# Hash attention and a SwiGLU block: three moved pieces of work at the seam between the two halves

## The chip, the cores and the metric

The kernel runs on one core of one Trainium2 chip. The metric is the device time of one execution in microseconds (us). Four runs of the kernel before gave 958.33, 955.05, 956.46 and 951.87 us, a median of 955.76.

## The reference, cut to what matters

```python
# q, k, v: (4, 8, 768, 64); proj: (64, 6)
q_bits = (q @ proj) > 0; k_bits = (k @ proj) > 0        # six sign bits a row
mask = (bucket(q_bits)[:, :, :, None] == bucket(k_bits)[:, :, None, :])
scores = where(mask, q @ k.T / 8, -1e9)
attn = softmax(scores) @ v                              # float32
x = attn, laid out as (4 * 768, 512)
g = x @ w_gate                                          # 512 x 1536, given as float64
out = ((g * sigmoid(g)) * (x @ w_val)) @ w_out          # 1536 x 512
```

The weights arrive as float64, and the matmuls of the second half are done to nearly float32 accuracy: each operand is cut into a high part, a low part and their difference, so that every product costs three matmuls.

## The kernel before, in words

**Two halves on one core.** `attention` goes over 16 pairs of heads (4 batches of 4 pairs, n = 0 to 15; `NP` = 4). `gated_block` then goes over the 4 batches: for each, twelve up blocks (`("U", f)`, 128 columns of both w_gate and w_val) and four down products (`("D", n)`, three up blocks' worth of w_out). Their order is written out in `order`: U0 U1 U2 U3 D0 U4 U5 U6 D1 U7 U8 U9 D2 and so on.

**A pair of attention.** TensorE (PE) makes scores in 24 groups (line 471), ScalarE (ACT) takes the exponentials (474), VectorE (DVE) adds them up (503, 507), PE multiplies by v (485). The sums of a pair are made one pair later by `total`: four pairs of matmuls with ones (518), a copy to `row` (521) and a small DMA few<-row (523) on SP's queue. `invert` takes reciprocals and spreads them by way of DRAM (sums, then r, 536); `norm` scales x by them (542, DVE), and for batches 1 to 3 sends x to DRAM (xram<-xT, 547). The lists `waiting`, `last` and `left` carry these closures on to later places. From pair 4 on the next pair's q and k are transposed on DVE (438); their hash bits go through ACT (402) and a spread (411 on DVE for k, a DMA qb<-qb, 414, on SP for q).

**Preparing the weights.** w_gate, w_val and w_out are cut into 36 pieces of 128 by 512 numbers. A piece goes through: a load (`words`, line 122); two scalings on ACT (130, 131); three steps on DVE (`widths`: 144, 146, 149); a rounding on ACT (137, `round_up`); two steps on DVE (`parts`: 157, 159); and a write to DRAM, ram<-stage (161), 768 KB. The stage tile of a piece is one of three buffers (four in attention), so the scaling of piece i waits until the write of piece i - 3 has landed. 24 pieces are prepared within attention, by `begin_pieces(count)` and `advance_pieces` once a pair; the other 12 within the first batch of the gated part. There the generator `preparing` hands out one DVE step at a time (five for each piece), and `scale_ahead` issues the scalings of the next piece when the counts allow.

**The gated part.** A prepared piece comes back to SBUF by a ring load, ring<-ram (232), 768 KB, issued by GpSimd; the ring has seven tiles, and `bring` loads the next one when one has been used. An up block makes, for gate and then for value, 16 matmuls into `a` and 8 into `n` (both at line 632). ACT evicts `a` (674), DVE subtracts `n` (680); silu on ACT (682), a product on DVE (684), and hid is cut into parts by ACT (685) and DVE (688, 690, the `tail`). A down product goes over six chunks; a chunk is six matmuls into `t[:, 0]` and three into `t[:, 1]`, which are evicted by ACT (719, first product of a batch) or DVE (721) and then a subtraction on DVE (724). All these PSUM tiles (a, n, o) come from one pool of four, taken in turn.

**What sets the order.** There is no scheduler: each engine runs its instructions in the order in which Python issues them. In the gated part one "atom" is issued (an up block's half, or a chunk), then the tail of the block before, then one preparing step, then `scale_ahead`:

```python
            for atom in atoms_of(kind, n):
                tail = atom()
                finish(tails)
...
                prepare_on(1)
                scale_ahead()
```

Ahead of U9 of a batch (`f == NF - NQ`) the next batch's x is fetched into the buffers that `words` used, so all preparing steps that are left are issued there in one go:

```python
                if f == NF - NQ and b + 1 < B:
                    while next(preparing, None):
                        pass
```

In the last down product of all, the first two thirds of four chunks are issued ahead (`ahead = 4`), and the rest of each chunk after them.

Of the kernel before, what the change touches and what calls it, by code (L numbers as in the profile page):

```python
# [13 lines left out]
ALU = mybir.AluOpType  # L14
# [5 lines left out]
def kernel(  # L20
# [35 lines left out]
    NQ = 3  # L56
# [108 lines left out]
    def begin_pieces(count):  # L165
        for i in sorted(added - rounded):
            round_up(i)
        for i in range(progress["scaled"], min(progress["scaled"] + count, NPIECE)):
            load_words(i + 1)
            scale(i)  # L170
# [50 lines left out]
    def bring(count=1):  # L221
        for _ in range(count):
            i = len(held)
            if i == len(wanted):
                return
            what, n = wanted[i]
            at = place[what, n % NF]
            while progress["kept"] <= at:
                next(preparing)
            pool = ringp[i % sum(RINGS) >= RINGS[0]]  # L230
            held[what, n] = t = pool.tile([P, 3, PIECE], FP32R, tag="ring", name="ring")
            nc.gpsimd.dma_start(t.bitcast(FP32), ram[at].bitcast(FP32))  # L232
# [23 lines left out]
    def attention(scope):  # L256
# [306 lines left out]
        for n in range(len(pairs)):  # L563
            u = 2 * NCH * n
            more = n + 1 < len(pairs)
            late = n + 1 > NP
            if n and more:
                steps = front(n + 1)
                if late:
                    prepare_pair(2)  # L570
            for i in range(2 * NCH):
                score(u + i)
                if u + i == 2:
                    prepare_pair(1)
                    finish(rest)
                    steps = front(n + 1)
                if i % NCH:
                    add(u + i)
                if late and i == 2:
                    load(n + 2, "qk")  # L580
            if more and not late:
                prepare_pair(4)
                load(n + 2, "qk")
            if n:
                total(n - 1)
            if more:
                prepare_pair(1)
            finish(rest)
            finish(last)
            while waiting:  # L590
                last.append(waiting.pop(0)())
            begin_pieces(0 if n == len(pairs) - 1 else 2 if n < NP or n % 2 else 1)
            for c in range(NCH):
                attend(u + c)
            finish(splits)
            for c in range(NCH, 2 * NCH):
                attend(u + c)
            load(n + 2, "v")
            advance_pieces()
            if n >= len(pairs) - 3:  # L600
                bring(2 if n == len(pairs) - 1 else 1)
        finish(last)
        total(len(pairs) - 1)
        left.extend(waiting)

    left = []
# [8 lines left out]
    def gated_block(scope):  # L615
# [47 lines left out]
        def atoms_of(kind, n):  # L663
            if kind == "U":
                b = n // NF
                hid = hids[n] = hidp.tile([P, 3, S], FP32R, tag="hid", name="hid")
                h, l, d = (hid[:, i] for i in range(3))
                gate, val = (gatep.tile([P, S], FP32, tag=name, name=name) for name in "gv")
                ops = {}
                for what, z in (("g", gate), ("v", val)):  # L670
                    def one(what=what, z=z):
                        ops[what] = up(n, what)
                        ops[what][0]()
                        nc.scalar.activation(two(z), ops[what][2], AF.Copy, scale=STEP + 1)  # L674

                    def other(what=what, z=z):
                        _, second, _, n_ = ops[what]
                        second()
                        bring()
                        nc.vector.tensor_tensor(two(z), two(z), n_, op=ALU.subtract)  # L680
                        if what == "g":
                            nc.scalar.activation(z, z, AF.Silu)  # L682
                            return
                        nc.vector.tensor_tensor(val, gate, val, op=ALU.mult)  # L684
                        nc.scalar.activation(h, val, AF.Copy, scale=TOWARD / STEP)  # L685

                        def tail():
                            nc.vector.scalar_tensor_tensor(out=l, in0=h.bitcast(FP32), scalar=-STEP,  # L688
                                                           in1=val, op0=ALU.mult, op1=ALU.add)
                            nc.vector.tensor_tensor(d, h.bitcast(FP32), l.bitcast(FP32),  # L690
                                                    op=ALU.subtract)

                        return tail

                    yield one
                    yield other
            else:
                b, part = divmod(n, NF // NQ)
                ws = [held["o", NQ * n + j] for j in range(NQ)]
                hs = [hids[NQ * n + j] for j in range(NQ)]  # L700
                tiles = {}

                def start(c, js):
                    if c not in tiles:
                        tiles[c] = two_banks("o")
                    t = tiles[c]
                    cols = slice(c * P, (c + 1) * P)
                    for j in js:
                        for v in range(2):
                            mm(t[:, 0], hs[j][:, v, cols], ws[j][:, v],  # L710
                               j == 0 and v == 0, j == NQ - 1 and v == 1)
                    for j in js:
                        mm(t[:, 1], hs[j][:, 2, cols], ws[j][:, 2], j == 0, j == NQ - 1)

                def end(c):
                    t = tiles.pop(c)
                    if part == 0:
                        accs[c] = outp.tile([P, DM], FP32, tag=f"o{c}", name="o")
                        nc.scalar.activation(accs[c], t[:, 0], AF.Copy, scale=STEP + 1)  # L719
                    else:  # L720
                        nc.vector.scalar_tensor_tensor(out=accs[c], in0=t[:, 0],  # L721
                                                       scalar=STEP + 1, in1=accs[c],
                                                       op0=ALU.mult, op1=ALU.add)
                    nc.vector.tensor_tensor(accs[c], accs[c], t[:, 1], op=ALU.subtract)  # L724
                    if part == NF // NQ - 1:
                        nc.sync.dma_start(rows[b][:, c, :], accs[c])
                    if c == NCH - 1:
                        bring(NQ)

                ahead = 4 if n == B * NF // NQ - 1 else 0  # L730
                for c in range(ahead):
                    yield lambda c=c: start(c, range(NQ - 1))
                for c in range(NCH):
                    def chunk(c=c):
                        start(c, [NQ - 1] if c < ahead else range(NQ))
                        end(c)
                    yield chunk
# [6 lines left out]
        for kind, n in order:  # L744
            if kind == "U":
                b, f = divmod(n, NF)
# [3 lines that stand above are left out]
                    splits = [None] * 4  # L750
                    for pr in range(NP):
                        t = wordp.tile([P, PIECE, 2], I32, tag="words", name="words")
                        x = t.rearrange("p f w -> p (f w)")[:, 0:S].bitcast(FP32)
                        nc.sync.dma_start(x, kept_x[b + 1, pr])
                        splits += split(x, b + 1, pr, xs[(b + 1) % 2][pr])
            if kind == "D" and n == B * NF // NQ - 1:
# [4 lines that stand above are left out]
                if tail:  # L761
                    tails.append(tail)
                if splits:
                    step = splits.pop(0)
                    if step:
                        step()
                count[0] += 1
                if left and count[0] in (6, 14):
                    left.append(left.pop(0)())
                    left[:] = [f for f in left if f]  # L770
                prepare_on(1)
                scale_ahead()

    with ExitStack() as scope:
# [33 lines left out]
```

## Time and profile before

| | |
|---|---|
| median of four runs | 955.76 us |
| the profiled execution: its own time, its span | 958.33 us, 956.6 us |
| TensorE busy | 928.3 us, 97% of the span, 5413 matmuls |
| VectorE busy | 672.8 us, 70% |
| ScalarE busy | 472.9 us, 49% |
| mean granted TensorE clock | 0.995 |
| DMA | 203.22 MB, a mean of 212 GB/s |
| attention | 0 to 340.66 us (first gated matmul) |
| first batch's D0, D1, D2 | from 378.02, 415.52 and 460.76 us |

The profile is one execution. "Busy" counts an engine's instructions, not its waits; a wait is written in square brackets behind the instruction that had to wait, with what released it. In a table of stretches, the figures behind the start and end are the length, the busy time of PE, its weight loads, DVE, ACT and GpSimd, then the granted PE clock, the share of the DMA engines and GB/s. In the chain, a line gives start, length and what it was.

### The profile page before, as it was taken

The numbers are of one execution on the slowest core, as the hardware profiler recorded it, in microseconds if no ns is written. First come the engines' busy times: TensorE is split into PE (matmuls) and PEld (weight loads), VectorE is DVE, ScalarE is ACT, GpSimd is POOL, SyncE is SP. The second block draws the span as 40 slices with busy tenths as digits, with TensorE's granted clock in tenths as the row PEclk, the third lists the DMA queues.
The fourth block names the chain that finished last, engine by engine and source line by source line (L and its number), as shares of the span: only waits on it lengthen the run. The fifth ranks groups of instructions, "written<-read, shape, count | busy, mean of one in ns | idle before, by whom it ended". The sixth has DMA issues, their size and how long they took to land.

```text
span 956.6 us, 14590 instructions
## 1 busy us (share of the span) xinstructions
PE 928.3 (97%) x5413; PEld 728.9 (76%) x5413; DVE 672.8 (70%) x868; ACT 472.9 (49%) x882; POOL 113.2 (12%) x231
## 2 busy tenths in 40 slices
PE   8999999999999999999799999999999999999997
PEld 3444455444554478989599999999999999999996
DVE  5577899888898828787876546775646586446466
ACT  6899777887887735534242331332332422332311
POOL 3011001000011020111011011011111111110100
PEclk9999999999999999999899999999999999999999
DMA  6466667888788598879677475466654645753641
GB/s 166 124 187 177 182 169 197 216 207 185 199 228 210 191 342 293 320 266 362 236 247 280 163 255 182 166 239 221 257 200 158 234 183 196 267 198 132 240 156 66
DMA packets 135798, 203.22 MB, mean 212 GB/s; under 512 B 92912, under 2 KB 100560, under 8 KB 135728
## 3 DMA queue, kind: packets, MB, share of 16 engines
q0 software_dynamic: 27984, 145.64, 43.0%
q1 hardware_dynamic: 106944, 56.46, 22.3%
q8 instruction: 43, 0.70, 0.3%
q10 hardware_dynamic: 800, 0.20, 0.1%
q14 instruction: 27, 0.22, 0.1%
HBM read 162.01 MB, written 39.42 MB: 211 GB/s over the span
## 4 chain that ended last, share of the span: by engine, by line
PE 65%; DVE 12%; SPq 8%; DMA 7%; ACT 4%; issue 4%; DVEq 0%; ACTq 0%; POOLq 0%
PE a L632 22%; PE o L632 18%; PE n L632 11%; PE sc L471 8%; SPq L296 7%; PE av L485 4%; DMA ram<-stage 3%; DVE acc L507 2%; ACT A L474 1%; DVE o L724 1%; DMA qb<-qb 1%; DVE stage L146 1%; DMA r<-sums 1%; DVE stage L157 1%; PE hps L397 1%
## 5 line engine op out<-in xcount | busy, mean ns | idle before, releaser
L632 PE MATMUL a<-xparts,ring 128*128 128x384 f32 x1536 | 282.6, 335 | 3.7 <-ACT g L674 2.7
L632 PEld LDWEIGHTS a<-xparts,ring 128*128 128x128 f32 x1536 | 267.9, 188 | 6.6 <-ACT g L674 3.3
L632 PE MATMUL o<-ring,hid 128*128 128x512 f32 x864 | 201.7, 393 | 7.5 <-ACT g L674 7.4
L632 PEld LDWEIGHTS o<-ring,hid 128*128 128x128 f32 x864 | 162.8, 189 | 42.5 <-ACT g L674 7.7
L474 ACT ACTIVATE A<-sc 128x384 f32<-128x384 f32 x384 | 156.1, 508 | 14.0 <-PE sc L471 13.9
L471 PE MATMUL sc<-qT,kT 64*128 64x384 f32 x768 | 160.2, 492 | 0.0
L632 PE MATMUL n<-xparts,ring 128*128 128x384 f32 x768 | 148.6, 335 | 0.0
L232 POOL DMA_DIRECT2D ring<-ram x144 | 75.9, 529 | 511.9 <-PE n L632 313.9
L632 PEld LDWEIGHTS n<-xparts,ring 128*128 128x128 f32 x768 | 134.5, 188 | 0.0
L507 DVE TENSOR_TENSOR acc<-acc,A 128x768 f32<-128x768 f32 x128 | 122.7, 958 | 13.7 <-DVE acc L503 0.5
L485 PE MATMUL av<-A,vraw 128*64 128x386 f32 (+1 forms) x768 | 127.7, 489 | 0.0
L680 DVE TENSOR_TENSOR v<-v,n 128x768 f32<-128x768 f32 x48 | 45.8, 954 | 101.8 <-PE n L632 95.9
L471 PEld LDWEIGHTS sc<-qT,kT 64*128 64x128 f32 x768 | 75.3, 188 | 49.6 <-issue 45.6
L485 PEld LDWEIGHTS av<-A,vraw 128*64 128x64 f32 x768 | 53.7, 137 | 73.3 <-issue 63.8
L674 ACT ACTIVATE g<-a 128x768 f32<-128x768 f32 x48 | 38.8, 808 | 127.9 <-PE a L632 127.9
L685 ACT ACTIVATE hid<-v 128x768 fp32r<-128x768 f32 x48 | 40.6, 847 | 117.7 <-DVE v L684 111.0
L682 ACT ACTIVATE g<-g 128x768 f32<-128x768 f32 x48 | 40.7, 847 | 92.1 <-DVE g L680 92.1
L471 PE MATMUL sc<-qb,kb 64*128 64x384 bf16 x384 | 73.5, 325 | 8.9 <-DVE kb L411 4.8
L724 DVE TENSOR_TENSOR o<-o 128x512 f32<-128x512 f32 x96 | 66.0, 687 | 22.0 <-ACT o L719 19.5
L688 DVE SCALAR_TENSOR_TENSOR hid<-hid,v 128x768 fp32r<-128x768 f32 x48 | 45.9, 957 | 31.6 <-ACT hid L685 31.6
L680 DVE TENSOR_TENSOR g<-g,n 128x768 f32<-128x768 f32 x48 | 45.6, 949 | 31.2 <-PE n L632 29.8
L721 DVE SCALAR_TENSOR_TENSOR o<-o 128x512 f32<-128x512 f32 x72 | 49.5, 687 | 12.0 <-PE o L632 11.4
(77 smaller groups left out, 672.8 us busy)
## 6 DMA issues: line engine op xcount, KB each, us to landing
ring<-ram POOLq DMA_DIRECT2D x144, 768.0 KB, 5.6
ram<-stage POOLq DMA_DIRECT2D x24, 768.0 KB, 4.5
ram<-stage SPq DMA_DIRECT2D x12, 768.0 KB
vraw<-in_v_dram SPq DMA_DIRECT2D x16, 384.0 KB
out_dram<-o SPq DMA_DIRECT2D x24, 256.0 KB
r<-sums SPq DMA_DIRECT2D x30, 192.0 KB
qraw<-in_q_dram SPq DMA_DIRECT2D x48, 96.0 KB
words<-in_moe_w_gate_dram POOLq DMA_DIRECT2D x9, 512.0 KB, 7.5
```

The costliest lines, as they stand in the source:

```text
L232: nc.gpsimd.dma_start(t.bitcast(FP32), ram[at].bitcast(FP32))
L296: queue.dma_start(blocks[at : at + BLOCK], src[b, 2 * pr + h][:, x * BLOCK : (x + 1) * BLOCK].rearrange("(a p c) d -> p c a d", c=NCH, p=B ...
L471: nc.tensor.matmul(sc[h], x["k", n][rows, ks], x["q", n][rows, qs], start=start, stop=not start)
L474: nc.scalar.activation(weights(u)[:, h, 0:HQ], sc[h], AF.Exp, scale=SCALE * (OFF / 2 if n <= NP else 1.0))
L485: nc.tensor.matmul(ps[h * D : (h + 1) * D, 0:width], raws["v", n][:, h, c, :], a[:, h, 0:width], start=c == 0, stop=c == NCH - 1)
L507: nc.vector.tensor_tensor(acc[n, half], acc[n, half], a[:, :, 0:HQ], op=ALU.add)
L632: nc.tensor.matmul(ps, w, x, start=start, stop=stop)
L680: nc.vector.tensor_tensor(two(z), two(z), n_, op=ALU.subtract)
L682: nc.scalar.activation(z, z, AF.Silu)
L688: nc.vector.scalar_tensor_tensor(out=l, in0=h.bitcast(FP32), scalar=-STEP, in1=val, op0=ALU.mult, op1=ALU.add)
L721: nc.vector.scalar_tensor_tensor(out=accs[c], in0=t[:, 0], scalar=STEP + 1, in1=accs[c], op0=ALU.mult, op1=ALU.add)
L724: nc.vector.tensor_tensor(accs[c], accs[c], t[:, 1], op=ALU.subtract)
```

## The change

There are four edits. `begin_pieces` starts one piece in pair 5 instead of two, and two in pair 6 instead of one; the sum over all pairs stays at 24. After the last pair, `total(15)` is issued ahead of `finish(last)`, which holds the scaling of x of pair 14 (`norm`) and its DMA to DRAM; on SP, few<-row then stands ahead of xram<-xT. Beside a chunk of a down product two preparing steps are issued instead of one. And in the very last down product each chunk issues its three difference matmuls (`t[:, 1]`) ahead of the other six, and DVE subtracts them ahead of the scaled addition of `t[:, 0]`. No instruction is added or taken away on PE, DVE, GpSimd or SP; lines move by 6 to 10 in the later part of the file.

```diff
-            begin_pieces(0 if n == len(pairs) - 1 else 2 if n < NP or n % 2 else 1)
+            begin_pieces(0 if n == len(pairs) - 1 else 2 if n < NP or n % 2 and n > NP + 1 or n == NP + 2 else 1)
...
+        total(len(pairs) - 1)
         finish(last)
-        total(len(pairs) - 1)
         left.extend(waiting)
...
                     cols = slice(c * P, (c + 1) * P)
-                    for j in js:
-                        for v in range(2):
-                            mm(t[:, 0], hs[j][:, v, cols], ws[j][:, v],
-                               j == 0 and v == 0, j == NQ - 1 and v == 1)
-                    for j in js:
-                        mm(t[:, 1], hs[j][:, 2, cols], ws[j][:, 2], j == 0, j == NQ - 1)
+                    def first():
+                        for j in js:
+                            for v in range(2):
+                                mm(t[:, 0], hs[j][:, v, cols], ws[j][:, v],
+                                   j == 0 and v == 0, j == NQ - 1 and v == 1)
+
+                    def second():
+                        for j in js:
+                            mm(t[:, 1], hs[j][:, 2, cols], ws[j][:, 2], j == 0, j == NQ - 1)
+
+                    for go in (second, first) if final else (first, second):
+                        go()
 
                 def end(c):
                     t = tiles.pop(c)
+                    if final:
+                        nc.vector.tensor_tensor(accs[c], accs[c], t[:, 1], op=ALU.subtract)
                     if part == 0:
...
-                    nc.vector.tensor_tensor(accs[c], accs[c], t[:, 1], op=ALU.subtract)
+                    if not final:
+                        nc.vector.tensor_tensor(accs[c], accs[c], t[:, 1], op=ALU.subtract)
...
-                ahead = 4 if n == B * NF // NQ - 1 else 0
+                final = n == B * NF // NQ - 1
+                ahead = 4 if final else 0
...
-                prepare_on(1)
+                prepare_on(2 if kind == "D" else 1)
                 scale_ahead()
```

## The prediction

> **What bounds the kernel now.** I read the page first, then PE's waits, the order in time around them, and the chain.
>
> ```profile
> span 956.6 us, 14590 instructions
> PE 928.3 (97%) x5413; PEld 728.9 (76%) x5413; DVE 672.8 (70%) x868; ACT 472.9 (49%) x882; POOL 113.2 (12%) x231
> ```
>
> PE is busy for 928.3 of 956.6 us, so only the 28 us in which it stands still, and its slow stretches, can be won. From 475 us PE runs without a pause to 951; what matters lies before. PE's waits between 340 and 480 us:
>
> ```profile
> PE o L632 <- ACT g L674: 7.4, 1, 7.4
> PE a L632 <- ACT g L674: 2.7, 2, 2.5
> ```
>
> The first of them, in order of time:
>
> ```profile
> 456.59 0.66 ACT L130 ACTIVATE stage<-words 128x512 f32<-128x512 f32 x1 [4.01 <-DMA ram<-stage]
> ...
> 459.92 0.79 ACT L674 ACTIVATE g<-a 128x768 f32<-128x768 f32 x1
> 460.76 14.55 PE L632 MATMUL o<-ring,hid 128*128 128x512 f32 x54 [7.41 <-ACT g L674]
> ```
>
> At U9 (the tenth of the first batch's twelve up blocks) the code runs all preparing steps that are left, in one go. ACT stands in order behind scalings (L130), each waiting until a piece's write to DRAM (ram<-stage) frees one of three stage buffers; the eviction of g is behind them, and PE waits for it from 453.35 to 460.76: 7.4 us. The next 54 matmuls take 14.55 us where the later sets of the chain take 12.28, because the clock fell:
>
> ```profile
> 458.00:460.76 2.76, 0.00 (x0) 0.00 (x0) 2.59 (x5) 1.66 (x3) 0.00 (x0) 0.50 0.86 274
> 460.76:465.00 4.24, 4.24 (x10) 2.88 (x11) 3.90 (x5) 0.24 (x1) 0.00 (x0) 0.52 0.90 332
> ```
>
> PEclk (the seventh figure) is 0.50 from about 4.6 us after PE stopped until 465. The jam costs 7.4 + 2.3 = 9.7 us.
>
> The second wait is at the start of the gated part:
>
> ```profile
> 348.52 0.32 SPq L547 DMA_DIRECT2D xram<-xT  x1
> 348.94 0.59 SPq L523 DMA_DIRECT2D few<-row  x1
> 358.47 0.84 ACT L685 ACTIVATE hid<-v 128x768 fp32r<-128x768 f32 x1 [6.67 <-DMA words<-in_moe_w_out_dram]
> 360.06 3.05 PE L632 MATMUL a<-xparts,ring 128*128 128x384 f32 x16 [2.47 <-ACT g L674]
> ```
>
> The first hid tile lies where attention's tiles were, and by the program's waits its first writer needs both of these DMAs landed (the view guesses a third). The landing records give 355.29 for xram<-xT and 358.29 for few<-row; ACT goes on at 358.47, and PE lost 2.47 us.
>
> **The change, part by part.** The sum is against the profiled execution (958.33 us, span 956.6 and 1.7 around it), 2.6 us above the median of the four runs, 955.76; I carry the difference over to the median. Runs of one kernel spread over 951.87 to 958.33, so 0.5% (4.8 us) is about what can be told from no change.
>
> *One piece from pair 5 to pair 6.* DVE then does three widths steps less at the end of pair 5 (144, 146, 149: 1.78 us from 145.38 to 147.16). PE's wait for kb at 160.24 (1.49 us) goes. But pair 7 gets two parts steps more (1.33 us) before its transposes; the q and k loads on SP stand behind the transposes and the spread of qb behind those, and PE waits for qb at 180.70 (0.90 us) and 200.75 (0.51 us). By pair 9 the chain is where it was: 0, with -1.2 to +0.7 us for the range.
>
> *Sums ahead of the scaling of x.* few<-row then leaves at 340.7, when row is copied (340.13 + 0.48), instead of behind the scaling that waits until 347.48 for r. On SP it stands ahead of xram<-xT only; both are on one queue and it is 6 KB. hid then waits for xram<-xT alone: 355.3, 3.0 us earlier. ACT's g is out at 357.0, PE ends its block at 357.6 and does not wait: -2.5 us, and part of the two small waits behind (0.40 and 0.22): -2.9 us, from -2.4 to -3.1.
>
> *Differences first in the last down product.* In both orders DVE's first step on a chunk waits for the chunk's last matmul (the program sets one semaphore count for the whole tile), and two DVE steps of 0.69 us follow. Nothing is won at the end. PE needs the hid's difference (ready at 944.07) at the first late matmul instead of the third, but the 24 matmuls ahead end at 944.46. Cost 0; if that cover failed, about 0.4 us.
>
> *Steps doubled beside down products.* In the changed order D0 and D1 carry six steps more each, and of the jam's twelve DVE steps one remains. The jam goes: -9.7 us. So does D1's wait of 0.5. What comes instead I follow along the changed order, with the durations of before (spacing on DVE 0.60 for 128x512, 1.0 for 128x768).
>
> D0 (PE 378.02 on). Before the second chunk's subtraction stand two steps, so it ends at 388.9, not 388.3; the sixth chunk needs its PSUM tile: +0.6 us, and D0 ends at 391.2. ACT's round-up of a piece now stands ahead of the eviction of the fourth chunk and waits for a step that ends at 391.1. So the fourth chunk is done on DVE at 393.1, and the step behind it ends piece 27, which SP sends off at 393.75 (ram<-stage; before at 395.47). Now the crucial order: behind the sixth chunk ACT has the scaling of piece 30, which needs the buffer of piece 27, and only behind it the eviction of U4's g. Before, that eviction stood ahead of the scaling. PE goes through U4 until 399.55 and then needs that PSUM tile.
>
> When does piece 27 land? The three ring loads of 768 KB that D0's end releases leave at 391.2. Rows of before for a write that leaves soon after such a triple:
>
> ```profile
> 395.47 13.13 DMA ram<-stage
> 430.43 6.84 DMA ram<-stage
> 437.26 3.82 issue
> ```
>
> 13.1 us for one sent 4.9 us behind the triple, 10.6 us (landing record 441.01, ACT goes on at 441.08) for one 2.2 us behind it. Without a triple it is short: sent at 388.94, landed 392.18, 3.24 us. Piece 27 now leaves 2.55 us behind the triple; I take 10.6, with ends 3.2 and 13.1. It lands at 404.35; the two scalings (start to start 0.57 each, with waits 1.2) and the eviction (0.80) bring PE to 406.4: +6.9 us. As after the jam, the clock falls 4.6 us into that wait and stays low for 6.8: +2.3 us.
>
> The Trainium skill, DMA: Bandwidth & Descriptors, section Queues, rings and completion order, says that each engine takes turns between the queues that have work. By that a 768 KB write beside ring loads at half of some 400 GB/s would take an estimated 4 us and about 2 of latency, land at about 400, and cost some 2 us with no fall of the clock; the sum would be some 7 us lower. The rows of before differ: between 392.5 and 396.5 the DMA moved 366 GB/s, and by the packet records all of it was ring loads, while a load that SP had issued at 392.32 had not begun.
>
> D1. The wait in U5 lets DVE catch up, so its six chunks come in time. Piece 32 is ready 15.3 us into D1, 3 us behind the next triple, and with 10.6 lands at 25.9. ACT's scaling of piece 35 waits for it, and behind it stand 0.57 + 0.57 of scaling, silu (0.85) and v's eviction (0.80); PE wants v's tile at 25.2 and gets it at 28.8: +3.6 us, and 0.4 for U8's first tile. Ends 0 and 6.
>
> Sum: -9.7 - 0.5 - 2.9 + 0.6 + 6.9 + 2.3 + 4.0 = +0.7 us. Of the median: 956.5 us.
>
> **The rivals.**
>
> *Writes land in time* (faster). If HBM writes in D0 land in 3.2 us as the one at 388.94 did, U5 costs nothing: -9.2. Then DVE has not caught up at D1: by the same counting the sixth chunk waits 1.6, U7's tiles 0.4, 1.1 and about 1.5, +4.6, and U8 about 1.5 instead of 4.0. Sum +0.7 - 9.2 + 4.6 - 2.5 = -6.4: 949.4 us. For it: the DMA stands idle from 386.5 to 389.5 (share 0.06), and the next load of words leaves with the triple, not behind it. Against: both rows behind a triple took over 10 us.
>
> *The jam moves and grows* (slower). One mechanism: ACT stands in order behind a scaling whose buffer is not free. With 13.1 us for piece 27 (lands 406.9) U5's wait is 2.5 us longer, though PE then starts later in the slow stretch (-1.3); with the same for piece 32, U8's wait is 6.1, over 4.6, and the clock falls there too (2.6): +0.7 + 2.5 - 1.3 + 2.5 + 2.6 = +7.0: 962.8 us. It decides where landings take over some 11.6 us, from which U8's wait passes 4.6. For it: the row of 13.13 us. Against: PE that stands issues no ring loads, so the queue empties sooner than it did before.
>
> *Only the sums count.* If the step order did as much harm as good exactly, what stays is the -2.9 of the sums: 952.9 us, within the bound; it is part of the first case.
>
> **How the numbers follow.** An even trade, within 4.8 us either way, 0.45: the big terms, 13.1 off and 13.8 on, come from one mechanism (ACT behind a scaling) and are of one size. Landing in time 0.31: it needs one duration that no row behind a triple shows, but every smaller stall leans that way, and the sums' gain is nearly sure. Grown jam 0.24. The range: from 2 us below the faster case, for pair 6's 1.2 and part of the D1 stalls, 947; to 963, near the slower case; some 2 in 10 lie outside. The likeliest case's own range is 951.7 to 961.
>
> **What would show it.** Right: PE's wait of 7.4 for g at the third D is gone and its 54 matmuls take 12.3 us; ACT's hid goes on near 355.3; a wait of PE for g's eviction of some 7 us at U5, with PEclk 0.50 behind it, and in the chain ram<-stage of about 10 us ahead of it; a shorter one at U8. The last 54 matmuls and the two DVE steps behind them are unchanged. Wrong: no wait of PE over 2 us between D0 and D1 (then the faster case), or hid still held to 358 (then few<-row was not what held it), or two falls of the clock.

## The result, and the profile after

The changed kernel takes 958.18 us (median of 53 runs, 955.40 to 960.91), the kernel before 955.00 us (79 runs, 950.44 to 960.41): the ratio is 1.0032, with a 95% interval from 1.0024 to 1.0040. The change costs about 3 us and stays within the 0.5% that count here as no change. The two profiled executions alone would say the opposite, 956.45 us after and 958.33 before: single executions of one kernel differ by more than the change is worth, so medians are compared below, and profiles are read by stretches.

PE's waits after, from 335 to 480 us (us in total, times, longest):

```profile
PE a L632 <- ACT g L674: 7.9, 3, 6.2
PE a L632 <- ACT v L674: 3.7, 2, 3.4
```

The wait of 7.4 us ahead of D2 is not there; two others are. In the order of time (start, length, the operation, and in brackets the wait ahead of it):

```profile
334.94 0.59 SPq L523 DMA_DIRECT2D few<-row  x1
343.90 0.32 SPq L547 DMA_DIRECT2D xram<-xT  x1
...
351.60 0.84 ACT L685 ACTIVATE hid<-v 128x768 fp32r<-128x768 f32 x1 [4.44 <-DMA xram<-xT]
353.20 3.07 PE L632 MATMUL a<-xparts,ring 128*128 128x384 f32 x16 [1.48 <-ACT g L674]
...
397.14 0.66 ACT L130 ACTIVATE stage<-words 128x512 f32<-128x512 f32 x1 [6.74 <-DMA ram<-stage]
...
398.25 0.81 ACT L674 ACTIVATE g<-a 128x768 f32<-128x768 f32 x1
399.11 4.84 PE L632 MATMUL a<-xparts,ring 128*128 128x384 f32 x16 [6.18 <-ACT g L674]
...
444.09 0.66 ACT L130 ACTIVATE stage<-words 128x512 f32<-128x512 f32 x1 [5.18 <-DMA ram<-stage]
446.79 4.62 PE L632 MATMUL a<-xparts,ring 128*128 128x384 f32 x16 [3.37 <-ACT v L674]
...
460.98 12.44 PE L632 MATMUL o<-ring,hid 128*128 128x512 f32 x54
```

few<-row now leaves 9 us ahead of xram<-xT, and the first hid waits for xram<-xT alone. At 397.14 and 444.09 ACT starts a scaling (L130) that has waited for a write, with an eviction behind it that PE waits for: 6.18 us at the sixth up block (U5) and 3.37 us at the ninth (U8). D2 at 460.98 has no wait, and its 54 matmuls take 12.44 us instead of 14.55. The chain shows the two writes that ACT stood behind:

```profile
386.95 10.09 DMA ram<-stage
433.30 10.68 DMA ram<-stage
```

And the 16 matmuls behind each of the two waits take 4.84 and 4.62 us, where they take 3.0 at full clock. In the table of stretches (the seventh figure is PEclk):

```profile
392.78:396.20 3.42, 0.15 (x1) 0.00 (x0) 0.00 (x0) 0.00 (x0) 0.53 (x1) 1.00 1.02 424
396.20:399.61 3.41, 0.50 (x2) 0.50 (x3) 0.94 (x2) 1.92 (x3) 0.00 (x0) 0.50 1.03 418
399.61:403.03 3.42, 3.42 (x12) 3.42 (x12) 3.07 (x5) 2.06 (x3) 0.00 (x0) 0.50 1.04 395
...
443.99:447.40 3.41, 0.61 (x3) 0.62 (x4) 1.75 (x3) 2.64 (x4) 0.26 (x1) 1.00 1.01 398
447.40:450.81 3.41, 3.41 (x12) 3.41 (x12) 3.03 (x5) 2.06 (x3) 0.00 (x0) 0.50 0.25 103
```

The clock is low for 6.8 us from 396.20 on, within the first wait, and for 3.4 us behind the second.

### The profile page after: what moved, and what is told of

Same layout as the page of the kernel before. It is cut to its first block, busy times and chain, and to the rows that moved or that the text cites. A ratio compares the mean times of both kernels' runs of the same rounds, so it can differ in the third digit from the quotient of the medians.

```text
span 954.7 us, 14584 instructions
## 1 busy us (share of the span) xinstructions
PE 929.8 (97%) x5413; PEld 726.6 (76%) x5413; DVE 672.9 (70%) x868; ACT 472.9 (50%) x882; POOL 113.3 (12%) x231
## 4 chain that ended last, share of the span: by engine, by line
PE 74%; DVE 10%; DMA 6%; ACT 5%; issue 3%; SPq 2%; DVEq 0%; ACTq 0%
PE a L632 25%; PE o L632 17%; PE n L632 12%; PE sc L471 11%; PE av L485 7%; DMA ram<-stage 3%; DVE acc L507 3%; SPq L296 2%; ACT A L474 2%; PE hps L397 1%; DMA r<-sums 1%; DVE stage L146 1%; DMA xram<-xT 1%; PE sum L518 1%; PE tps L384 1%
## 5 line engine op out<-in xcount | busy, mean ns | idle before, releaser
L632 PE MATMUL a<-xparts,ring 128*128 128x384 f32 x1536 | 286.5, 338 | 12.6 <-ACT g L674 7.9
L632 PEld LDWEIGHTS a<-xparts,ring 128*128 128x128 f32 x1536 | 271.2, 190 | 16.6 <-ACT g L674 9.1
L632 PE MATMUL o<-ring,hid 128*128 128x512 f32 x864 | 199.4, 390 | 0.7 <-DVE o L733 0.7
L471 PEld LDWEIGHTS sc<-qT,kT 64*128 64x128 f32 x768 | 72.5, 189 | 48.5 <-issue 45.2
L733 DVE TENSOR_TENSOR o<-o 128x512 f32<-128x512 f32 x90 | 61.8, 687 | 22.4 <-ACT o L727 20.1
L471 PE MATMUL sc<-qb,kb 64*128 64x384 bf16 x384 | 69.0, 325 | 4.6 <-DVE kb L411 3.3
```

The lines of the kernel that those rows point to most:

```text
L471: nc.tensor.matmul(sc[h], x["k", n][rows, ks], x["q", n][rows, qs], start=start, stop=not start)
L632: nc.tensor.matmul(ps, w, x, start=start, stop=stop)
```

## The experiments

The theory at the start: the doubled steps trade the jam at D2 for waits at U5 and U8, because a write that leaves just behind the three ring loads (a "triple") that a down product's end releases is late, and ACT's in-order queue turns that into a wait of PE. Moving the last pair's sums (few<-row) ahead saves some 3 us; the other two edits do nothing. The rivals: attention or the last down product makes the difference, or the waits have another cause than those writes.

All results in one table. "Stretch" is the time from the first gated matmul to the end of D2's 54 matmuls in the one profile of that kernel; everything behind D2 takes 481 to 482 us in every profile. Ratios are against runs of the kernel before on the same chip.

| kernel | median, us | ratio, 95% interval | PE waits at the second block | at U5, U8 | ahead of D2 | stretch, us |
|---|---|---|---|---|---|---|
| before | 955.00 | 1 | 2.47 | none | 7.41 | 134.7 |
| pairs_alone | 953.88 | 0.9994 (0.9973 to 1.0016) | 6.06 | none | 4.56 | 136.4 |
| last_alone | 955.79 | 1.0002 (0.9981 to 1.0022) | 5.78 | none | 4.03 | 135.8 |
| sums_alone | 952.39 | 0.9969 (0.9949 to 0.9989) | 0.91 | none | 7.10 | 133.3 |
| steps_alone | 961.12 | 1.0052 (1.0032 to 1.0072) | 5.01 | 7.63, 2.71 | none | 141.8 |
| without_steps | 952.74 | 0.9967 (0.9945 to 0.9989) | 0.26 | none | 7.05 | 132.9 |
| after | 958.18 | 1.0032 (1.0024 to 1.0040) | 1.48 | 6.18, 3.37 | none | 138.6 |
| order_later | 954.83 | 0.9996 (0.9972 to 1.0020) | 0.64 | 1.36 in U5, 2.17; 1.84 in D1 | none | 135.8 |
| write_first | 950.96 | 0.9956 (0.9939 to 0.9974) | 1.59 | 1.91, 2.89; 1.86 in D1 | none | 134.0 |
| both_writes_first | 949.14 | 0.9932 (0.9908 to 0.9957) | 1.39 | 1.82, none | none | 129.0 |
| loads_in_place_on_sp | 955.14 | 0.9988 (0.9968 to 1.0007) | 0.55 | none; 5.66 at U6 | none | 134.4 |
| loads_behind_both | 953.47 | 0.9962 (0.9941 to 0.9983) | 1.40 | none; 3.16 in D1 | none | 131.8 |
| both_single_steps | 951.36 | 0.9955 (0.9938 to 0.9972) | 1.27 | none | 4.89 | 130.7 |

### Each part by itself

**pairs_alone.** Only the number of pieces in pairs 5 and 6:

```diff
-begin_pieces(0 if n == len(pairs) - 1 else 2 if n < NP or n % 2 else 1)
+begin_pieces(0 if n == len(pairs) - 1 else 2 if n < NP or n % 2 and n > NP + 1 or n == NP + 2 else 1)
```

> The kernel before with the changed numbers of pieces in pairs 5 and 6 alone. Theory (an even trade in the gated part sets the result, attention moves by 1 us at most): 953.8 to 955.7 us, the waits for kb at pairs 7 and 8 gone or smaller, the gated part unchanged with its 7.4 us wait at the third down product. Rival (attention gains what the doubled steps lose, since the profile of after reaches the gated part about 5 us earlier than that of before): 950 us.

0.9994, from -2.6 to +1.5 us: no gain of 5 us hides in attention. That the profile of after reaches the gated part 5.9 us sooner than that of before is mostly spread: the first gated matmul came at 336.03 to 340.66 us in the four profiles with the old numbers of pieces and at 334.70 to 339.15 in the nine with the new ones, up to 4.6 us apart with the same numbers. This is why the two profiled executions gave the wrong sign; the stretch of after, which leaves attention out, is 3.9 us longer. The profile of pairs_alone showed something else. This kernel still has the old order of few<-row, and its first hid ran much later than in the profile of before:

```profile
344.28 0.32 SPq L547 DMA_DIRECT2D xram<-xT  x1
344.70 0.59 SPq L523 DMA_DIRECT2D few<-row  x1
...
356.08 0.84 ACT L685 ACTIVATE hid<-v 128x768 fp32r<-128x768 f32 x1 [8.54 <-DMA few<-row]
357.68 5.24 PE L632 MATMUL a<-xparts,ring 128*128 128x384 f32 x16 [6.06 <-ACT g L674]
...
455.89 15.21 PE L632 MATMUL o<-ring,hid 128*128 128x512 f32 x54 [4.56 <-ACT g L674]
```

hid starts 21.4 us after the first gated matmul (334.70), in the profile of before 17.8. The other two kernels with the old order agree with this one: 21.1 in last_alone, 20.3 in steps_alone. The profile that the prediction was made from was the odd one out: its wait of 2.47 us is usually 5 to 6, with slow clock behind it (5.24 us for 16 matmuls). In the two of them that still have the wait ahead of D2, that one is shorter (4.0 and 4.6 us instead of 7.4), so part of the loss comes back; where the new order of few<-row makes the first wait 0.91 or 0.26 us, the one ahead of D2 is 7.10 or 7.05.

**sums_alone.** Only `total(len(pairs) - 1)` ahead of `finish(last)`:

```diff
+        total(len(pairs) - 1)
         finish(last)
-        total(len(pairs) - 1)
```

> The kernel before with the last pair's sums ahead of the scaling of x alone. As predicted: -2.9 us, 952.1 us, the first hid running at about 355 on the time axis of before. As the profile of after shows it (PE's wait at the second block 1.48 us instead of 2.47, hid then held by xram<-xT): -1.0 us, 954.0 us. Rival (the later stalls take it back): 955.0 us.

0.9969, -3.0 us (-4.9 to -1.1): the predicted -2.9, and not the -1.0 that comparing the one profile of before with the one of after gives. Its rows are those of after, 16.2 us from the first gated matmul (337.21) to hid:

```profile
346.30 0.32 SPq L547 DMA_DIRECT2D xram<-xT  x1
...
353.44 0.84 ACT L685 ACTIVATE hid<-v 128x768 fp32r<-128x768 f32 x1 [3.87 <-DMA xram<-xT]
355.04 3.05 PE L632 MATMUL a<-xparts,ring 128*128 128x384 f32 x16 [0.91 <-ACT g L674]
```

**steps_alone.** Only the doubling:

```diff
-                prepare_on(1)
+                prepare_on(2 if kind == "D" else 1)
```

> The kernel before with the steps doubled beside down products alone. Theory (jam gone, but ACT stands in order behind a scaling at the first two down products): by the rows of after -7.4 -2.3 -0.6 +0.3 +6.2 +2.1 +0.3 +3.4 +1.9 = +3.9 us, 958.9 us, from 957 to 960, with a wait of 5 to 8 us for g's eviction at the sixth up block. Rival (the doubling is even, and the loss comes from attention or from the last down product): 955 us within 1.

1.0052, +5.0 us (+3.1 to +6.9), somewhat more than the +3.9 expected, which the interval holds. The wait ahead of D2 is gone, U5 waits 7.63 us and U8 2.71:

```profile
405.36 5.28 PE L632 MATMUL a<-xparts,ring 128*128 128x384 f32 x16 [7.63 <-ACT g L674]
```

The loss is here, as the theory said.

**last_alone.** Only the order within the last down product:

```diff
-                    for j in js: ... t[:, 0]
-                    for j in js: ... t[:, 1]
+                    for go in (second, first) if final else (first, second):
+                        go()
```

> The kernel before with the changed order in the last down product alone. Theory (DVE's first step on a chunk waits for the whole chunk in both orders): no change, 955 us within 1. Rival (the parts taken alone gave -0.6, -3.0 and +5.0 us, +1.4 in all, and the whole change +3.1, so that 1.7 us come from here): 956.9 us, with a longer way from the end of the last matmul to the last store.

1.0002 (-1.8 to +2.1 us): nothing. In the profiles of before and after, the span ends 5.16 and 5.14 us behind the last matmul (951.44 to 956.6, 949.56 to 954.7), and 5.07 us behind it in that of last_alone (950.03 to 955.1).

**without_steps.** The changed kernel with `prepare_on(1)` everywhere.

> The changed kernel with one preparing step beside each down product's chunk, as before; the other three parts stay. Theory (the parts add up): 955.2 - 0.6 - 3.0 = 951.6 us, which would put the doubling at 6.6 us within the change, 1.6 more than it cost alone. Rival (the doubling costs the same 5.0 us in the change as alone): 953.2 us.

0.9967, -3.2 us (-5.3 to -1.1): what the sums and the pairs give together. Against this kernel the doubling makes the change 5.4 us slower by the medians, 6.2 by the ratios; alone it cost 5.0. The intervals are too wide to tell the two expectations apart, and the parts add up to the whole (-0.6 - 3.0 + 5.0 + 0.2 = +1.6, with an uncertainty of about 2 on each, against +3.1).

### Why PE waits at U5

**write_first.** The changed kernel, with two of the three ring loads moved onto SP's queue, where in this order they stand behind the writes of pieces 27 and 28:

```diff
                     if c == NCH - 1:
-                        bring(NQ)
+                        bring(1 if n == 0 else NQ)
...
                 scale_ahead()
+                if (kind, n, k) == ("D", 0, NCH - 1):
+                    bring(NQ - 1, nc.sync)      # ring loads issued by SP
```

> The changed kernel, but two of the three ring loads that the end of the first down product releases are issued by SP, behind the write of piece 27, instead of ahead of it. Theory (the write is late because it stands behind three ring loads): it lands 3 to 6 us after its issue instead of 10.1, PE's wait of 6.2 us at the sixth up block falls below 1.5 us and the fall of the clock behind it goes: 958.2 - 7 = 951 us (949.5 to 953). Rival (the write is slow for a reason of its own): 10 us as before and 958 us.

0.9956; 950.96 us, 7.2 less than the changed kernel. The chain has the same write with one ring load ahead of it instead of three:

```profile
387.93 5.82 DMA ram<-stage
```

and PE's wait at U5 falls from 6.18 to 1.91 us, without slow clock:

```profile
395.82 3.04 PE L632 MATMUL a<-xparts,ring 128*128 128x384 f32 x16 [1.91 <-ACT g L674]
```

The loads are the cause of the late write, and the late write of the wait. The wait is not below 1.5 us as expected, and a new one stands in D1 (1.86 us, with 3.81 us behind it for nine matmuls that take 2.34 at full clock).

How the loads delay the write can be read from the packets. SP had sent a load of words (512 KB, in packets of 1 KB) at 384.52, ahead of the write of 386.95. In the profile of after, the ring loads (q0) and what SP had sent (q1) moved the following from 387 to 391 us, and then from 392 to 396 (packets, MB, share of the DMA engines' time):

```profile
q0 software_dynamic: 212, 1.20, 84.1%
q1 hardware_dynamic: 285, 0.29, 20.7%
...
q0 software_dynamic: 183, 0.95, 57.0%
q1 hardware_dynamic: 178, 0.77, 46.2%
```

In the first stretch SP's queue moved more packets than the ring loads but a quarter of their bytes: they were the small packets of the words. The write's own first packet went at 391.30, 4.35 us after it was sent, and its last at 396.26. In write_first they went 2.64 and 5.08 us after it was sent. So part of the delay passes through a load that stands ahead of the write in SP's own queue; what sending that load later would gain, no run shows. At the second triple no such load was left, and the write sent at 433.30 still had its first packet at 437.48: from 433 to 437 us the ring loads moved and nothing of SP's.

**order_later.** The changed kernel, with the scaling of piece 30 kept behind the evictions of U4's g and v:

```diff
-                prepare_on(2 if kind == "D" else 1)
-                scale_ahead()
+                if (kind, n) == ("U", NQ + 1):
+                    prepare_on(0 if k < 2 else 2)
+                else:
+                    prepare_on(2 if kind == "D" else 1)
+                if (kind, n, k) != ("D", 0, NCH - 1) and not ((kind, n) == ("U", NQ + 1) and k < 2):
+                    scale_ahead()
```

> The changed kernel, but the scaling of piece 30 stands on ACT behind the evictions of the fifth up block's g and v instead of ahead of them; the two preparing steps of those two places are taken two places later. Theory (PE waits because that eviction is queued behind a scaling, not because data are late): the wait of 6.2 us for g at the sixth up block and the 2.1 us of slow clock behind it go, while the write may still take 10 us; DVE's steps come later and may hold PE for 1 to 2 us: 958.2 - 7 = 951 us (950 to 953). Rival (all of the chain is late with the write): 957 us or more.

954.83 us, between the two. U5's wait for g is gone, so the order on ACT is one half of the mechanism. But the writes were still late: that of piece 27, sent at 388.96, landed at 400.36, and the next one took 13.6 us in the chain. DVE's next preparing step waited for the scaling, and the subtraction of U4's v stood behind that step:

```profile
401.16 0.43 DVE L144 TENSOR_SCALAR stage<-stage 128x512 int32<-128x512 int32 x1 [5.84 <-ACT stage L130]
...
402.23 0.95 DVE L680 TENSOR_TENSOR v<-v,n 128x768 f32<-128x768 f32 x1
```

PE then waited 1.36 us for that subtraction (in U5) and 1.42 for g's eviction at 406.32, and U8's wait and the slow clock behind it stayed. The expected 951 was missed since only ACT's queue was thought of, and DVE's counted at 1 to 2 us.

**both_writes_first.** As write_first, at the second down product too:

```diff
-                        bring(NQ)
+                        bring(1 if n < 2 else NQ)
...
+                if kind == "D" and n < 2 and k == NCH - 1:
+                    bring(NQ - 1, nc.sync)
```

> The changed kernel with two of the three ring loads behind the writes at the end of the first down product, as in write_first (951.0 us), and also at the second. Theory (the wait of 2.9 us for v at the ninth up block has the same cause): the write sent just behind the second triple lands in 4 to 6 us instead of 10.2, that wait goes: 948.5 us (947.5 to 950). Rival (DVE's lag holds PE there in place of ACT): 951 us.

949.14 us: 0.9932 of before (0.9908 to 0.9957), the fastest kernel here, faster than both that the case began with. U8's wait is gone. The two largest of PE's waits that are left from 335 to 480 us:

```profile
PE a L632 <- ACT g L674: 3.4, 3, 1.8
PE o L632 <- DVE o L733: 0.7, 1, 0.7
```

**loads_in_place_on_sp** and **loads_behind_both.** All three loads on SP, at the first down product behind one write, or behind two:

```diff
-                        bring(NQ)
+                        bring(NQ, nc.sync if n < 2 else None)      # in place
...
-                    bring(NQ - 1, nc.sync)
+                    bring(NQ, nc.sync)                             # behind both, bring(0) in place
```

> The changed kernel; all three ring loads that the ends of the first and second down product release are issued by SP, where they stand in the program: at the first, behind the write of piece 27 and ahead of that of piece 28. Theory (a write is late when it stands behind ring loads, and each late one that a scaling waits for costs PE): piece 27 lands in 3.5 to 5 us and PE's wait at the sixth up block goes, but piece 28's write takes 9 us or more and PE waits about 3 us later, at the sixth or seventh up block: 951 us (949 to 953). Rival (only the first write matters, its reader being the scaling ahead of g's eviction): 947.5 us.

> The changed kernel; all three ring loads at the ends of the first and second down product are issued by SP behind the next writes (of pieces 27 and 28 at the first, as far as piece 32 at the second). Theory: piece 27 lands in 3.5 to 5 us instead of 5.8, the wait of 1.8 us at the sixth up block and the slow clock behind it (1.6 us) go, the ring is deep enough: 947 us (945.5 to 949) where two loads behind gave 949.1. Rival (the loads come 9 us later and PE waits for a ring tile at the seventh up block): 952 us.

955.14 and 953.47 us, both worse than two loads behind. In the first, U5's wait is gone, but the write of piece 28 left at 392.18, right behind the three loads, and ACT's next scaling came 15.9 us later, with v's eviction behind it:

```profile
408.08 0.66 ACT L130 ACTIVATE stage<-words 128x512 f32<-128x512 f32 x1 [9.58 <-issue]
...
410.77 4.62 PE L632 MATMUL a<-xparts,ring 128*128 128x384 f32 x16 [5.66 <-ACT v L674]
```

(The view names no releaser; by the program's waits the scaling needed this write, whose landing record is at 408.00, 15.8 us after it was sent.) That is the wait that was expected, of 5.7 us and slow clock instead of 3. In the second, U5 does not wait, but the loads leave at 397.5 with the next write behind them:

```profile
405.26 14.14 DMA ram<-stage
```

and PE stands 3.16 us within D1. The rival, PE short of ring tiles, is not seen: no wait of PE names a ring load. In both, the write that came next behind the three loads was late (15.8 and 14.1 us, in the second with a load of words ahead of it as well); what helped was to have no write that is soon needed stand behind them. Standing ahead of loads does not make every write quick: in both_writes_first that of piece 28, sent at 392.45 ahead of the two loads on SP's queue, took 8.96 us in the chain, but PE's next wait behind it was one of 0.64 us at 430.33.

**both_single_steps.** As both_writes_first, with one step beside each chunk.

> As both_writes_first (949.1 us), but with one preparing step beside each chunk, as in without_steps (952.7 us). Theory (the doubling is worth something once the writes go ahead of the ring loads; without it the jam of 7 us and 2 to 3 of slow clock at the third down product are still there): 952.7 us within 1.5. Rival (the gain comes from the order of the loads alone, with or without the doubling): 949 us.

951.36 us, 0.9955 (0.9938 to 0.9972); a wait of 4.89 us ahead of D2 is back, shorter than in without_steps. Beside 949.14 (0.9932, 0.9908 to 0.9957) the doubling is worth 2.2 us once the writes go first, with intervals that overlap. The median lies at the lower edge of the theory's range (951.2 to 954.2), and the jam is back but smaller than expected: the order of the loads gives part of its gain without the doubling.

## Why the prediction was right, point by point

The forecast of an even trade held: +0.7 us predicted (956.5), +3.1 measured (958.18), within the bound and the range. Term by term:

- *Jam.* Gone, with the slow clock behind it, as counted: 9.7 us by the profile of before (9.5 if the 14.55 us are set against the 12.44 of the same view). In pairs_alone and last_alone it was some 7 us (waits of 4.56 and 4.03, and 15.21 and 15.47 us for the 54 matmuls), in sums_alone 10: it is dear where the second block waits little. D1's wait of 0.5 is gone too, and D0's sixth chunk waits 0.65 where 0.6 was predicted.
- *Sums.* -2.9 predicted, -3.0 measured. The size is right by luck as much as by working. "hid then waits for xram<-xT alone" is right, but "355.3, 3.0 us earlier" is 14.6 us after the first gated matmul, and hid came 15.6 to 17.0 us after it in the kernels with the new order; "PE ... does not wait" failed too, it waits 0.3 to 1.6 us. The old order in turn usually costs more than its profile showed, 20 to 21 us instead of 17.8, and part of it comes back ahead of D2. The two errors cancel roughly.
- *Pairs and last down product.* 0 and 0 predicted; -0.6 (-2.6 to +1.5) and +0.2 (-1.8 to +2.1) measured.
- *U5.* "I take 10.6" for the landing: 10.09. +6.9 for the wait: 6.18. +2.3 for the clock: 4.84 us for sixteen matmuls against 3.04 at full clock, so 1.8; but it fell 3.3 us into the wait, not "4.6 us into that wait". This was the crucial order, and write_first shows its cause. (Before, the write behind the first triple took 13.13 us and PE did not wait in U5: the scaling that needed it stood behind the eviction of U5's g. That write is on the chain that leads to the jam, all the same.) The rival in which writes land in time fell with it: 10.09 and 10.68 us, where the turns between queues, as the Trainium skill's page DMA: Bandwidth & Descriptors (Queues, rings and completion order) has them, were worked out to about 6. Once the write of piece 27 moved, the packets do look like turns (178 against 183 from 392 to 396 us) and it took 5 us; the estimate left out the 4.35 us before its first packet, with a load ahead of it in its own queue. The 4.18 us before the first packet at the second triple, with no such load, are not explained by turns.
- *U8.* 10.6 for the landing: 10.68. +3.6 for the wait: 3.37. The +0.4 for U8's first tile did not come; a wait of 0.30 stands in U7 instead, for DVE's last step on D1. What was missing is the clock: the 16 matmuls behind it take 4.62 us, about 1.6 more than at full clock. The prediction had put the threshold at a wait of 4.6 us ("over 4.6, and the clock falls there too"); here it fell behind a wait of 3.37. This is the mis-sized term that the rows show.
- *The sum.* By the runs the doubling costs 5.0 us alone and 5.4 to 6.2 within the change, where the terms (-9.7 - 0.5 + 0.6 + 6.9 + 2.3 + 4.0) make +3.6. U8's slow clock fills most of that difference; the rest is within the intervals, and it stays open. By the stretches of single profiles the doubling costs 5.4 to 7.1 us alone (141.8 against 136.4, 135.8 and 134.7) and 5.3 to 5.7 within the change (138.6 against 133.3 and 132.9).

## What to carry to other kernels

Before work is moved to an idle engine or a quieter place, ask what its last step waits for: here the step that gained nothing for PE (a scaling waiting for a buffer that a DMA frees) stood in order ahead of an eviction that PE needed, and doubling the pace brought it there sooner than the DMA could free the buffer. Loads that were released several at once delayed a write that something was waiting for, in part through a smaller load ahead of it in its own queue; issuing that write first was worth 7 to 9 us against the changed kernel, more than any edit of the change. And one profile is one draw: a wait of 2.5 us in it was 5 to 6 in three others with the same order of instructions there, so a term read from one profile should be checked against a second one where it can be had.

## What the runs showed of the hardware

The granted clock falls on a grid, not a fixed time after PE stops. All stretches of 0.50 clock between start and end of these profiles last 3.41, 6.83 or 10.24 us, and within a profile they begin whole multiples of 3.413 us apart (after: 140.20, 396.20 and 447.40, 75 and 15 steps). Two waits of about one length, in both_writes_first (1.82 us) and write_first (1.91 us), show what that means. Stretches cut on each one's grid (to 0.1 us), of both_writes_first:

```profile
391.98:395.39 3.41, 1.59 (x10) 1.27 (x9) 1.64 (x3) 1.90 (x3) 0.53 (x1) 1.00 0.95 284
395.39:398.80 3.41, 3.41 (x13) 3.41 (x12) 3.06 (x5) 2.06 (x3) 0.00 (x0) 0.51 1.03 409
```

and of write_first:

```profile
391.55:394.97 3.42, 2.37 (x14) 2.04 (x12) 2.26 (x4) 1.11 (x2) 0.53 (x1) 1.00 1.04 334
394.97:398.38 3.41, 2.56 (x15) 2.56 (x16) 2.27 (x5) 2.39 (x5) 0.00 (x0) 1.00 0.91 329
```

In the first the wait lies within one window, PE is busy for 1.59 of it, and the next window runs at half clock, where 16 matmuls take 4.60 us instead of 3.04; in the second it lies across a border, neither window is that empty, and nothing happens. There is no sharp limit in how much PE worked. In all thirteen profiles, from 10 us on to the last matmul, every window at full clock with PE busy for less than 1.6 us was followed by a fall; of those with 1.65 to 1.92 us some were (sums_alone, 136.79: 1.92) and some were not (write_first, 442.83: 1.65), and none with more was. So waits of 1.8 to 3.4 us cost themselves and, by where they lay on the grid, 1.3 to 1.6 us more (1.82, 1.86, 2.17 and 3.37 us) or nothing (1.91, 2.47, 2.71 and 2.89). The Trainium skill, TensorE: Matmul & The Clock Gate, Part 1 on the HAM clock gate, states a free-running window of 4096 cycles at 1.2 GHz, 3413 ns; these profiles agree with it (steps of 3.413 us). For U8 it means that no fixed time from the stop of PE, such as the 4.6 us that the prediction read from one row, decides whether the clock falls.
